# Attention, top-1 experts and a Winograd-form feed-forward on one core: the last stage's block sums spread over the steps, gates applied to the tokens on ACT, weight conversion given out by a budget of DVE work

## The chip, the core and the metric

One NeuronCore of a Trainium2 chip runs the whole program in one launch; the other cores are idle. The metric is the device time of that launch in microseconds (us). Of the kernel before there are three timed runs, given with their median, and one profiled execution, which has a time of its own.

## The reference, cut to what matters

```python
out = q @ (k^T v)                              # 8 batches, 8 heads, 576 rows, 64 dims, no softmax
x = out / sqrt(mean(out^2) + 1e-6) * g_norm    # 4608 tokens of 512
logits = norm(x) @ norm(expert_emb)^T / tau    # 8 experts
e = argmax(logits); gate = softmax(logits)[e]
x = gate * (relu(x @ w1[e]) @ w2[e])           # 512 -> 1024 -> 512, the token's expert alone
h = x @ w_in;  g = h * cos(h);  y = g @ w_out  # 512 -> 2048 -> 512, every token
```

The second feed-forward's weights come as float64. The gate is a softmax value and so positive.

## The kernel before, in words

Every product that has to be exact is made of three passes over split operands: a high half, and a low half that is the rest (`PASS`, L229). ACT makes the high half by a copy and DVE the low half by a subtraction.

The program has three stages.

1. Attention, normalisation, ranking of the tokens by expert, and scattering of the rows to `xs` in expert order.
2. The expert stage, the loop over `g` at L1347. There are 16 chunks of 304 tokens (`CH`, `NC`), each in 8 positions (`f`), so g = 8c + f. Position g issues `layer1` of (c, f), which is 12 matmuls into a PSUM bank `hps`, with a ReLU on ACT and the low half on DVE; then `layer2` of the position two before, 12 matmuls into the four banks `y`. `turn_x` transposes the next chunk's rows in positions 3 to 6. `gate_x` is a generator that computes the gate of a chunk's rows in small pieces, one a position, on ACT and DVE; it then writes the gates to DRAM and reads them back broadcast to 128 partitions (L208, L212). `store_y` multiplies the four `y` banks by that broadcast gate on DVE (L267) and `flush` stores them to `yT`. `load_x` (L158, POOL's queue) brings the rows `xr` of a chunk. Beside all this the loop converts the float64 weights of the third stage from their bits (`bits`, `convert`, `prepare`), a piece at a time: L1416 says by hand how many pieces a position gets, one to three.
3. The last stage: nine blocks of 512 tokens, each in eight steps, so steps 0 to 71, and two more to drain. The two layers are done in Winograd's form of a 2x2 block product, with seven products in place of eight. Step i (`step`, L1197) issues the seven hidden products of step i into the banks `ha` and `hb` ("h" units), and the six or seven output products of step i - 2 into banks `o_a11`, `o_s2` and so on ("o" and "t" units); `units` (L471) gives the order. Between them DVE and ACT form h cos(h), its sums and their halves. PE must have its `ha` or `hb` read by DVE or ACT before it writes it anew.

A block ends in a step that the code calls `done`. There DVE forms E1 = U2 + s3, a half of the output tile `o_sb`, and U2 + acc; in the first slot of the step after (`after`, L1254) it makes the two remaining sums, and POOL sends four sets of 128 rows to `out` by indirect DMAs (`out_rows`, L1171). After the last step these two sums and four DMAs end the program (L1480). Such an end of a block with the step after it is called a seam below.

```python
            if after:
                ...
                add(o2[:, :, 256:512], halves(E1), halves(bank[prior, "s1"]))
                add(o1[:, :, 256:512], halves(U2), halves(bank[prior, "s1"]))
                out_rows(prior, 0, o1)
                out_rows(prior, 1, o2)
```

Of the kernel before, what the change touches and what calls it, by code (L numbers as in the profile page):

```python
# [10 lines left out]
F32 = mybir.dt.float32  # L11
# [25 lines left out]
def tile_kernel(ctx, tc, q, k, v, g_norm, emb, tau, w1, w2, w_in, w_out, out):  # L37
# [36 lines left out]
    BY_POOL = 3  # L74
# [86 lines left out]
    def gate_x(c):  # L161
# [16 lines left out]
        for r in range(4):  # L178
# [5 lines left out]
            if r % 2:  # L184
# [13 lines left out]
        nc.scalar.activation(out=z, in_=z, func=ACTF.Exp)  # L198
        V.tensor_reduce(out=y, in_=z, axis=AX.X, op=ALU.add)
# [15 lines left out]
    def turn_x(c, k, ps=None):  # L215
        if k == 0:
            c["xT"] = [[P.xt.tile([128, CH], F32R, name=f"xT{a}{q_}", tag=f"xT{a}{q_}") for q_ in range(4)] for a in range(2)]
        p = P.ps_x.tile([128, 512], F32, name="xp", tag="xp") if ps is None else ps()
# [9 lines left out]

    PASS = ((0, 0), (0, 1), (1, 0))  # L229

    def layer1(c, f):
        w = c["w"](f)
        p = P.ps_h.tile([128, 512], F32, name="hps", tag="hps")
# [68 lines left out]
    def bits(raw, t, mk, out):  # L302
        lo, hi = raw[:, :, 0], raw[:, :, 1]
        hf = hi.bitcast(F32)
        nc.scalar.activation(out=mk, in_=hf, func=ACTF.Abs)
# [3 lines left out]
        yield 7  # L309
        V.scalar_tensor_tensor(out=t, in0=hi, scalar=-0x40000000, in1=t, op0=ALU.bitwise_and, op1=ALU.bitwise_or)  # L310
        yield 7
        V.scalar_tensor_tensor(out=out.bitcast(F32), in0=mk, scalar=TINY, in1=t.bitcast(F32), op0=ALU.is_gt, op1=ALU.mult)

    def convert(x):
        layer, m = CONV[x]
        if x == 0:
            convert_load(0)
            convert_load(1)
            for _ in range(4):
                yield 7  # L320
# [6 lines left out]
        yield 7  # L327
# [102 lines left out]
    def prepare(store, a, layer, q_):  # L430
# [7 lines left out]
        if layer == 0:  # L438
            sum_(s1, a21, a22, ALU.add)
            sum_(a21, a11, a21, ALU.subtract)  # L440
            yield 8
            sum_(s2, s1, a11, ALU.subtract)
            sum_(s4, a12, s2, ALU.subtract)
        else:
            sum_(s1, a12, a11, ALU.subtract)
            sum_(s4, a22, a12, ALU.subtract)
            yield 8
            sum_(s2, a22, s1, ALU.subtract)
            sum_(a12, a21, s2, ALU.subtract)
        yield 8  # L450
        t = WAB[0]
        store_some(7)
        for i, n, src in ((0, 2, a[:, 0:512]), (2, 2, a[:, 512:1024]), (4, 3, o)):
            src = src.rearrange("p (n c) -> p n c", n=n)
            split2(t[:, i:i + n, 0], t[:, i:i + n, 1], src)
            yield 3 * n + 1
        for u in range(7):
            if layer and (q_ or u not in KEPT):
# [12 lines left out]
    def units(i):  # L471
# [4 lines left out]
            h(A11, B11), h(S1, T1), o("a11", W11), h(S2, T2), h(S4, B22), o("a22", W4), h(S3, T3), o("s2", V2),  # L476
            h(A12, B21), o("a12", W21), h(A22, T4), *last, o("s3", V3), o("s1", V1),
# [78 lines left out]
    if True:  # L556
# [409 lines left out]
        for t in range(NTILE):  # L966
# [41 lines left out]
            if t == 29:  # L1008
# [6 lines left out]
                P.gs = pool("gs", 2, bctx, side="right")  # L1015
# [12 lines left out]
    if True:  # L1028
# [83 lines left out]
        def out_unit(o, j, name, w, start, stop):  # L1112
            for th in range(2):
                for n, (a, b_) in enumerate(PASS):
                    nc.tensor.matmul(  # L1115
                        out=o[:, th * 256:th * 256 + 256], lhsT=G[j, name][a][:, th * 128:th * 128 + 128], rhs=w[:, b_, 0:256],
                        start=(start and th == 0 and n == 0), stop=(stop and th == 1 and n == 2),
                    )
# [522 lines left out]
```

## Time and profile before

| | us |
|---|---|
| median of three runs | 1373.41 |
| lowest and highest run | 1369.27 and 1378.28 |
| the profiled execution's own time | 1374.12 |
| its span, first to last instruction | 1372.6 |
| mean granted TensorE clock | 0.991 |

The span is what the rows below divide. Busy time of PE is modelled: a matmul's row reaches into the next one's, so a full stretch shows PE busy all the time and says nothing of its rate. What the profile does show is where PE sits idle, and who ended each wait. PEld is PE's weight load; a wait can stand at PE's row, at PEld's, or at both, since one sequencer issues them.

### The profile page before, as it was taken

How to read it: one execution, taken by the hardware profiler on the slowest of the kernel's cores; microseconds unless marked ns; L12 is line 12 of the kernel's file. 1: busy time of each engine (PE TensorE's matmuls, PEld its weight loads, DVE VectorE, ACT ScalarE, POOL GpSimd, SP SyncE). 2: the span in 40 equal slices, each digit the busy share in tenths (PEclk: the TensorE clock that was granted, in tenths of full speed). 3: DMA queues.
4: the chain of work that ended last, by engine and by line, in shares of the span. 5: the costliest groups of instructions: out<-in, count | busy, mean ns of one | idle time of the engine just before them, and what ended most of it. 6: DMA issues, size and time to landing. Idle time of an engine off the chain costs nothing. (4 is left out here: it accounts for less than half of the span.)

```text
span 1372.6 us, 30155 instructions
## 1 busy us (share of the span) xinstructions
PE 1311.9 (96%) x10825; PEld 1283.7 (94%) x10825; DVE 1119.2 (82%) x2551; ACT 795.7 (58%) x1601; POOL 174.1 (13%) x302
## 2 busy tenths in 40 slices
PE   7997799999999999998999999999999999999995
PEld 6876789999999999998999999999999999999995
DVE  2567957899998988977888898888988888898874
ACT  4657435555555454546657666666666657666662
POOL 1244132313221100000000010100101010010101
PEclk9999999999999999999999999999999999999998
DMA  9998485899999998669988888988888888988882
GB/s 272 299 333 253 135 237 170 209 271 267 243 254 252 254 271 258 191 197 354 343 300 291 291 281 265 312 259 294 286 275 293 267 292 276 298 281 261 287 267 88
DMA packets 239749, 361.20 MB, mean 263 GB/s; under 512 B 27148, under 2 KB 117424, under 8 KB 238376
## 3 DMA queue, kind: packets, MB, share of 16 engines
q1 hardware_dynamic: 221928, 295.25, 70.0%
q0 software_dynamic: 17648, 63.91, 14.6%
q8 instruction: 89, 1.46, 0.4%
q14 instruction: 68, 0.56, 0.1%
q10 hardware_dynamic: 16, 0.02, 0.0%
HBM read 301.19 MB, written 57.91 MB: 262 GB/s over the span
## 5 line engine op out<-in xcount | busy, mean ns | idle before, releaser
L237 PE MATMUL hps<-xT,ring 128*128 128x304 f32 x1536 | 243.0, 306 | 6.5 <-DVE xT L226 3.3
L258 PE MATMUL y<-h,ring 128*128 128x304 f32 x1536 | 236.6, 302 | 4.3 <-DVE yo L267 1.6
L237 PEld LDWEIGHTS hps<-xT,ring 128*128 128x128 f32 x1536 | 219.6, 189 | 9.8 <-DVE xT L226 5.0
L258 PEld LDWEIGHTS y<-h,ring 128*128 128x128 f32 x1536 | 220.3, 188 | 5.6 <-issue 2.9
L1073 ACT ACTIVATE u<-u,half_pi 128x512 f32<-128x512 f32 x142 | 102.4, 721 | 57.9 <-DVE u L1070 51.7
L1174 POOL DMA_INDIRECT out<-o_sb,perm_i x36 | 39.3, 1091 | 703.0 <-DVE o_sb L1147 535.4
L1067 ACT ACTIVATE u<-h 128x512 int32<-128x512 f32 x142 | 89.8, 632 | 64.0 <-DVE h L1147 53.0
L1070 DVE SCALAR_TENSOR_TENSOR u<-h,u 128x512 f32<-128x512 f32 x142 | 98.1, 691 | 28.7 <-ACT u L1067 24.7
L243 ACT ACTIVATE h<-hps 128x304 fp32r<-128x304 f32 x128 | 53.7, 419 | 108.1 <-PE hps L237 108.0
L1115 PE MATMUL o_a<-ring,hi 128*128 128x256 f32 x568 | 107.8, 282 | 0.0
L1144 ACT ACTIVATE hi<-u 128x512 fp32r<-128x512 f32 x142 | 88.6, 624 | 25.8 <-DVE u L1150 22.8
L1150 DVE TENSOR_TENSOR lo<-u,hi 128x512 fp32r<-128x512 f32 x142 | 97.2, 685 | 0.0
L141 DVE TENSOR_TENSOR ring<-raw,ring 128x1024 fp32r<-128x1024 f32 x72 | 87.6, 1216 | 7.0 <-ACT ring L140 6.0
L1144 ACT ACTIVATE hi<-h 128x256 fp32r<-128x256 f32 (+1 forms) x142 | 73.8, 520 | 23.5 <-DVE h L1267 20.0
L1115 PEld LDWEIGHTS o_a<-ring,hi 128*128 128x128 f32 x568 | 87.1, 189 | 0.0
L1267 DVE TENSOR_TENSOR h<-h,u 128x512 f32<-128x512 f32 x71 | 49.0, 690 | 45.4 <-ACT u L1073 45.2
L1115 PE MATMUL o_a<-ring,lo 128*128 128x256 f32 x284 | 79.6, 280 | 0.0
L1150 DVE TENSOR_TENSOR lo<-h,hi 128x256 fp32r<-128x256 f32 (+1 forms) x142 | 78.3, 551 | 0.0
L140 ACT ACTIVATE ring<-raw 128x1024 fp32r<-128x1024 f32 x72 | 75.9, 1054 | 0.8 <-DMA raw<-in_moe_w 0.7
L244 DVE SCALAR_TENSOR_TENSOR h<-hps,h 128x304 fp32r<-128x304 f32 x128 | 59.6, 466 | 15.4 <-ACT h L243 15.3
L1115 PE MATMUL o_s<-ring,hi 128*128 128x256 f32 x372 | 70.0, 282 | 0.0
L1105 PE MATMUL ha<-ring,wb 128*128 128x256 f32 x390 | 58.3, 285 | 1.9 <-DVE h L1147 0.9
(323 smaller groups left out, 3222.7 us busy)
## 6 DMA issues: line engine op xcount, KB each, us to landing
wb<-ws SPq DMA_DIRECT2D x223, 256.0 KB
wa<-ws SPq DMA_DIRECT2D x167, 256.0 KB
raw<-in_moe_w SPq DMA_DIRECT2D x144, 256.0 KB
ring<-ws SPq DMA_DIRECT2D x114, 256.0 KB
wb<-wo SPq DMA_DIRECT2D x97, 256.0 KB
ring<-wo SPq DMA_DIRECT2D x74, 256.0 KB
wa<-wo SPq DMA_DIRECT2D x73, 256.0 KB
ws<-wa POOLq DMA_DIRECT2D x56, 256.0 KB
```

Source lines behind the costliest of these rows:

```text
L140: nc.scalar.activation(out=w[:, 0], in_=raw, func=ACTF.Copy)
L141: nc.vector.tensor_tensor(out=w[:, 1], in0=raw, in1=w[:, 0].bitcast(F32), op=ALU.subtract)
L237: nc.tensor.matmul(out=p[:, 0:CH], lhsT=w[:, a, k * 128:(k + 1) * 128], rhs=c["xT"][b_][k], start=(n == 0), stop=(n == 11),)
L244: V.scalar_tensor_tensor(out=lo, in0=p[:, 0:CH], scalar=0.0, in1=hi.bitcast(F32), op0=ALU.max, op1=ALU.subtract)
L258: nc.tensor.matmul(out=c["y"][d][:, 0:CH], lhsT=w[:, a, 512 + d * 128:512 + (d + 1) * 128], rhs=h[b_], start=(f == 0 and i == 0), stop=(f ...
L1067: nc.scalar.activation(out=n, in_=p, func=ACTF.Copy, scale=TURN, bias=0.25)
L1070: V.scalar_tensor_tensor(out=u, in0=p, scalar=TURN, in1=n, op0=ALU.mult, op1=ALU.subtract)
L1073: nc.scalar.activation(out=u, in_=u, func=ACTF.Sin, scale=2 * math.pi, bias=half_pi)
L1105: nc.tensor.matmul(out=out, lhsT=w[:, a, k * 128:(k + 1) * 128], rhs=x[xi][:, b_, k * 256:(k + 1) * 256], start=(start and n == 0), stop=( ...
L1115: nc.tensor.matmul(out=o[:, th * 256:th * 256 + 256], lhsT=G[j, name][a][:, th * 128:th * 128 + 128], rhs=w[:, b_, 0:256], start=(start an ...
L1144: nc.scalar.activation(out=out, in_=in_, func=ACTF.Copy)
L1150: V.tensor_tensor(out=out, in0=x, in1=y, op=ALU.subtract)
```

## The change

- The order of the output units becomes a11, s2, a12, s3, a22, s1. The sums of a block are put into five slots of two steps, and the last step is a function of its own, `last_step`, which goes over the tokens' two halves and sends each half's rows when it is done.
- From chunk 4 on the gate is multiplied into the token rows `xr` by ACT before they are transposed, instead of into `y` by DVE; ReLU lets a positive factor through. The gate's way through DRAM is gone for these 12 chunks, and `store_y` becomes four ACT copies. `gate_x` and `load_x` of a chunk start earlier (`GATE_AT`, `LOAD_AT`).
- `layer1` and `turn_x` take banks `hps` and `xp` in turn (`any_bank`) from g = 16 on.
- Conversion is given out by a budget: 32 units of DVE work a position, less what the rest of the position needs. ACT's `Abs` stands later within a piece, and 14 weight stores go by SP's queue in place of POOL's.

```diff
@@ gate_x
         V.tensor_scalar(out=mx, in0=n2, scalar1=1e-30, scalar2=None, op0=ALU.max)
+        if SCALED <= c["n"] < NC:
+            yield
         nc.scalar.activation(out=y, in_=mx, func=ACTF.Ln)
...
+        if SCALED <= c["n"] < NC:
+            yield
+            for r in range(4):
+                nc.scalar.activation(out=t[:, r, 0:DM], in_=t[:, r, 0:DM], func=ACTF.Copy, scale=gt[:, r:r + 1])
+            return
@@ store_y
-            V.tensor_tensor(out=o[d], in0=c["y"][d][:, 0:CH], in1=c["gate"], op=ALU.mult)
+            if "gate" in c:
+                V.tensor_tensor(out=o[d], in0=c["y"][d][:, 0:CH], in1=c["gate"], op=ALU.mult)
+            else:
+                nc.scalar.activation(out=o[d], in_=c["y"][d][:, 0:CH], func=ACTF.Copy)
@@ turn_x and layer1
+    turn = [-1]
+
+    def any_bank(name):
+        if turn[0] >= 0:
+            turn[0] += 1
+            name = ("hps", "xp")[turn[0] % 2]
+        p = P.ps_h if name == "hps" else P.ps_x
+        return p.tile([128, 512], F32, name=name, tag=name)
@@ prepare
-            if layer and (q_ or u not in KEPT):
+            if layer and (q_ or u not in KEPT) or not layer and q_ >= 6:
                 stores.append((store[u], t[:, u].rearrange("p a c -> p (a c)").bitcast(F32)))
@@ units
-            h(A11, B11), h(S1, T1), o("a11", W11), h(S2, T2), h(S4, B22), o("a22", W4), h(S3, T3), o("s2", V2),
-            h(A12, B21), o("a12", W21), h(A22, T4), *last, o("s3", V3), o("s1", V1),
+            h(A11, B11), h(S1, T1), o("a11", W11), h(S2, T2), h(S4, B22), o("s2", V2), h(S3, T3), o("a12", W21),
+            h(A12, B21), o("s3", V3), h(A22, T4), *last, o("a22", W4), o("s1", V1),
@@ step
+        def late_sum(b, t, x):
+            add(OUT[b][t][:, :, 256:512], halves(x), halves(bank[b, "s1"]))
+            for th in range(2):
+                out_row(b, t, th)
...
+        def last_step():
...
+            for th in range(2):
+                part = slice(th * 256, th * 256 + 256)
+                for kind, _, name, w in todo:
...
+                    else:
+                        for t, y in ((1, E1), (0, acc)):
+                            add(OUT[b][t][:, th, 256:512], y[:, part], x)
+                            out_row(b, t, th)
...
             if after:
-                prior = b - 1
-                o1, o2 = OUT[prior]
-                add(o2[:, :, 256:512], halves(E1), halves(bank[prior, "s1"]))
-                add(o1[:, :, 256:512], halves(U2), halves(bank[prior, "s1"]))
-                out_rows(prior, 0, o1)
-                out_rows(prior, 1, o2)
+                add(E1, U2, bank[b - 1, "s3"])
...
+            if after:
+                late_sum(b - 1, 1, E1)
...
+            if after:
+                late_sum(b - 1, 0, Y["acc"])
...
             if done:
-                add(E1, U2, bank[b, "s3"])
-                add(OUT[b][1][:, :, 0:256], halves(E1), halves(bank[b, "a22"]))
-                add(U2, U2, Y["acc"])
+                add(Y["acc"], U2, Y["acc"])
@@ the loop over g
+        preps, GATE_AT, LOAD_AT = [], {0: 0, OPEN + 2: 1, OPEN + 5: 2, 2 * OPEN: 3, 2 * OPEN + 3: 4}, {OPEN + 3: 3, 2 * OPEN: 4}
+        for n in range(5, NC):
+            GATE_AT[8 * n - 14] = LOAD_AT[8 * n - 17] = n
+        spare, FULL, CARRY = 0, 32, 15
+
+        def vector_work(c, f, splits):
+            w = 4 + 12 * splits + (6 if c >= NC - 2 else 14 if c == 2 else 0) + (16 if f == 1 and c < 5 else 0)
+            return w + (4 if 3 <= f < 7 else 0) + ({2: 4, 3: 28, 4: 2, 6: 10, 0: 5}.get(f, 0) if c < NC - 2 else 0)
...
+                spare = min(spare, CARRY) + FULL - vector_work(c, f, splits)
+                spent = 0
+                while spare - spent >= 3 and spent < 15:
+                    k = next(conv, 999)
+                    spent += abs(k)
+                    if k < 0:
+                        break
+                spare -= spent
```

DVE at the second seam, before: `e` is E1, `u_8713` is U2, `o_sb` the output tile, `sx` a sum for the next block's tokens, and the rest is the step's own work.

```order
L1147 TENSOR_TENSOR e_8712<-u_8713,o_s_10182 128x512
L1147 TENSOR_TENSOR o_sb_11185<-e_8712,o_a_10120 128x2x256
L1147 TENSOR_TENSOR u_8713<-u_8713,acc 128x512
L1070 SCALAR_TENSOR_TENSOR u_11228<-h,u_11228 128x512
L1147 TENSOR_TENSOR u_11165<-h 128x256
L1150 TENSOR_TENSOR lo_11241<-h,hi_11240 128x256
L1147 TENSOR_TENSOR o_sb_11185<-e_8712,o_s_10190 128x2x256
L1147 TENSOR_TENSOR o_sb_11184<-u_8713,o_s_10190 128x2x256
L376 TENSOR_TENSOR sx<-sx,xb_10946 128x512
L1267 TENSOR_TENSOR h<-h,u_11228 128x512
```

The same place now (E1 is `e_8724`, U2 is `u_8725`).

```order
L1169 TENSOR_TENSOR acc<-u_8725,acc 128x512
L1089 SCALAR_TENSOR_TENSOR u_11238<-h,u_11238 128x512
L1169 TENSOR_TENSOR u_11176<-h 128x256
L1172 TENSOR_TENSOR lo_11251<-h,hi_11250 128x256
L1169 TENSOR_TENSOR e_8724<-u_8725,o_s_10166 128x512
L395 TENSOR_TENSOR sx<-sx,xb_10958 128x512
L1325 TENSOR_TENSOR h<-h,u_11238 128x512
```

Ahead of the step's first own row (L1070, now L1089) stands one sum instead of three, and ahead of `sx` one instead of two.

DVE in the third and fourth slot of the same step, before: `h<-two,hb`, `h<-five,ha` and `h<-one,hb` are the reads of PE's banks.

```order
L1147 TENSOR_TENSOR h<-two,hb 128x256
L1150 TENSOR_TENSOR u_11228<-h,u_11228 128x256
L1150 TENSOR_TENSOR lo_11239<-h,hi_11238 128x512
L1150 TENSOR_TENSOR lo_11243<-u_11165,hi_11242 128x512
L1147 TENSOR_TENSOR h<-five,ha 128x256
L1147 TENSOR_TENSOR h<-one,hb 128x256
L1070 SCALAR_TENSOR_TENSOR u_11338<-h,u_11338 128x512
```

And now:

```order
L1169 TENSOR_TENSOR h<-two,hb 128x256
L1172 TENSOR_TENSOR u_11238<-h,u_11238 128x256
L1172 TENSOR_TENSOR lo_11249<-h,hi_11248 128x512
L1169 TENSOR_TENSOR o_sb_11197<-e_8724,o_a_10194 128x2x256
L1172 TENSOR_TENSOR lo_11253<-u_11176,hi_11252 128x512
L1169 TENSOR_TENSOR h<-five,ha 128x256
L1169 TENSOR_TENSOR o_sb_11197<-e_8724,o_s_10202 128x2x256
L1169 TENSOR_TENSOR h<-one,hb 128x256
L1089 SCALAR_TENSOR_TENSOR u_11335<-h,u_11335 128x512
L1169 TENSOR_TENSOR o_sb_11196<-acc,o_s_10202 128x2x256
```

One sum has come in ahead of `h<-five,ha`, one behind it, and one behind the `u` that follows `h<-one,hb`.

The end of DVE's program now, the second half of the last step (before, the eight sums there were of 128x512, the last two behind the last matmul's bank).

```order
L1169 TENSOR_TENSOR acc<-acc,hb 128x256
L1169 TENSOR_TENSOR u_8725<-e_8724,o_s_18381 128x256
L1169 TENSOR_TENSOR o_sb_19239<-e_8724,o_a_18404 128x256
L1169 TENSOR_TENSOR acc<-u_8725,acc 128x256
L1169 TENSOR_TENSOR e_8724<-u_8725,o_s_18430 128x256
L1169 TENSOR_TENSOR o_sb_19240<-e_8724,o_a_18458 128x256
L1169 TENSOR_TENSOR o_sb_19240<-e_8724,o_s_18466 128x256
L1169 TENSOR_TENSOR o_sb_19239<-acc,o_s_18466 128x256
```

The sums are half as wide, and only the last two need the bank that the last matmuls write.

ACT in the expert stage now, around positions 0 to 2 of a chunk: `h` is the ReLU, `yo` the copies of the finished chunk, `xr<-xr,gt` the gate's scaling of the next chunk and `gx<-xr` the squares of the one after.

```order
L259 ACTIVATE h_5494<-hps 128x304
L286 ACTIVATE yo<-y_5147 128x304
L286 ACTIVATE yo<-y_5148 128x304
L286 ACTIVATE yo<-y_5149 128x304
L286 ACTIVATE yo<-y_5150 128x304
L140 ACTIVATE ring_5518<-raw 128x1024
L364 ACTIVATE wa<-sa 128x2x256 x2
L364 ACTIVATE wa<-sb 128x3x256
L210 ACTIVATE xr<-xr,gt 76x512 x4
L259 ACTIVATE h_5544<-xp 128x304
L328 ACTIVATE c_mk<-c_raw 128x512
L174 ACTIVATE gx<-xr 76x512 x4
```

The `yo` and `xr` rows are new on ACT; between the two ReLUs stand eight instructions more than without them.

## Rows read from the trace of the kernel before

**Rows 1.** The page, busy time, share of the span and instructions of each engine.

```profile
PE 1311.9 (96%) x10825; PEld 1283.7 (94%) x10825; DVE 1119.2 (82%) x2551; ACT 795.7 (58%) x1601; POOL 174.1 (13%) x302
```

**Rows 2.** Stretches: length, PE, PEld, DVE, ACT, POOL busy, clock, DMA share, GB/s.

```profile
185.00:570.00 385.00, 382.10 (x2827) 380.14 (x2826) 340.50 (x799) 201.38 (x388) 73.75 (x139) 1.00 0.88 242
570.00:600.00 30.00, 28.04 (x204) 27.58 (x203) 27.12 (x79) 13.39 (x31) 0.00 (x0) 1.00 0.43 130
600.00:640.00 40.00, 35.85 (x263) 34.89 (x263) 27.14 (x62) 21.28 (x44) 3.85 (x7) 0.96 0.96 325
...
725.00:1357.30 632.30, 627.48 (x5201) 621.35 (x5200) 542.35 (x1076) 403.66 (x800) 30.71 (x28) 1.00 0.84 276
1357.30:1372.60 15.30, 0.00 (x0) 0.00 (x0) 2.46 (x4) 0.00 (x0) 3.90 (x4) 0.67 0.19 73
```

**Rows 3.** Waits of PE, 185 to 600 us: in total, times, longest us.

```profile
PE hps L237 <- DVE xT L226: 2.1, 5, 0.8
PE y L258 <- DVE yo L267: 1.6, 3, 1.1
PE y L258 <- ACT ring L382: 1.2, 1, 1.2
```

**Rows 4.** Waits of PE, 600 to 725 us.

```profile
PE hb L1105 <- DVE h L1147: 0.9, 1, 0.9
PE ha L1105 <- DVE h L1147: 0.9, 1, 0.9
```

**Rows 5.** Waits of PEld, 725 to 1360 us, the seams.

```profile
PEld hb L1105 <- DVE h L1147: 4.1, 6, 0.7
PEld ha L1105 <- DVE lo L1150: 2.7, 7, 0.4
PEld ha L1105 <- ACT h L1144: 1.9, 7, 0.3
```

**Rows 6.** Timeline of the second seam: start, length, engine, operation, [idle before].

```profile
796.53 0.72 ACT L1073 ACTIVATE u<-u,half_pi 128x512 f32<-128x512 f32 x1
...
797.09 0.68 DVE L1147 TENSOR_TENSOR o_sb<-e,o_s 128x512 f32<-128x512 f32 x1
...
798.28 0.68 DVE L376 TENSOR_TENSOR sx<-sx,xb 128x512 f32<-128x512 f32 x1
...
798.88 0.68 DVE L1267 TENSOR_TENSOR h<-h,u 128x512 f32<-128x512 f32 x1
...
800.28 0.41 DVE L1147 TENSOR_TENSOR h<-two,hb 128x256 f32<-128x256 f32 x1
...
802.16 0.41 DVE L1147 TENSOR_TENSOR h<-five,ha 128x256 f32<-128x256 f32 x1
```

**Rows 7.** Timeline of the end.

```profile
1356.95 0.28 PE L1115 MATMUL o_s<-ring,lo 128*128 128x256 f32 x1
...
1359.08 0.68 DVE L1147 TENSOR_TENSOR o_sb<-u,o_s 128x512 f32<-128x512 f32 x1
1360.03 0.97 POOL L1174 DMA_INDIRECT out<-o_sb,perm_i  x1 [64.17 <-DVEq L1513]
...
1363.87 0.97 POOL L1174 DMA_INDIRECT out<-o_sb,perm_i  x1 [0.30 <-issue]
```

**Rows 8.** Groups by line, 185 to 590 us: busy us, mean ns of one, idle before.

```profile
L243 ACT ACTIVATE h<-hps 128x304 fp32r<-128x304 f32 x115 | 48.3, 420 | 96.2 <-PE hps L237 96.1
...
L174 ACT ACTIVATE gx<-xr 76x512 f32<-76x512 f32 x60 | 32.8, 623 | 0.0
...
L225 ACT ACTIVATE xT<-xp,g 128x304 fp32r<-128x304 f32 x56 | 28.1, 503 | 5.4 <-PE xp L220 5.3
...
L267 DVE TENSOR_TENSOR yo<-y,gate 128x304 f32<-128x304 f32 x56 | 22.5, 462 | 4.0 <-DMA gate<-gates 4.0
```

**Rows 9.** Tile xr: durations, then first and last start.

```profile
L158 POOL DMA_DIRECT2D xr<-xs x16: 536/542/635, 133.6 to 526.7; - x16
...
L220 PEld LDWEIGHTS kvp<-ident,xr x8: 138/141/142, 139.7 to 141.6; 76*128 76x128 f32 x8
```

More of the change, by code (lines that the diff above doesn't have):

```diff
@@ L319, in convert @@
             for _ in range(4):
[L320 removed]
+                yield 2
         raw = cv.pop(x)
@@ L1113, in out_unit, with out_half, kept @@
             for th in range(2):
[L1114 to L1118, printed above, removed]
+                out_half(o, j, name, w, th, start and th == 0, stop and th == 1)
+        def out_half(o, j, name, w, th, start, stop, **kw):
+            for n, (a, b_) in enumerate(PASS):
+                nc.tensor.matmul(
+                    out=o[:, th * 256:th * 256 + 256], lhsT=G[j, name][a][:, th * 128:th * 128 + 128], rhs=w[:, b_, 0:256],
+                    start=(start and n == 0), stop=(stop and n == 2), **kw,
+                )
+        def kept(q, w):
+            if q == 0:
+                return WAB[0][:, w]
+            i = KEPT.index(w)
+            return WOUT[q][:, :, i * 256:i * 256 + 256]
         def out_product(u):
@@ L1169, in two_of, with out_row @@
             return x.rearrange("p (n c) -> p n c", n=2)
-        def out_rows(b, t, o):
-            for th in range(2):
-                n = 4 * b + 2 * t + th
-                ins = nc.gpsimd.indirect_dma_start(
-                    out=out, out_offset=bass.IndirectOffsetOnAxis(ap=perm_i[:, n:n + 1], axis=0),
-                    in_=o[:, th], in_offset=None, bounds_check=NT - 1, oob_is_err=False,
-                )
-                tc.add_to_no_dep_group("rows", ins.ins)
-                tc.declare_no_dep(ins.ins, group="rows", reason="every token has its own row")
+        def out_row(b, t, th):
+            n = 4 * b + 2 * t + th
+            ins = nc.gpsimd.indirect_dma_start(
+                out=out, out_offset=bass.IndirectOffsetOnAxis(ap=perm_i[:, n:n + 1], axis=0),
+                in_=OUT[b][t][:, th], in_offset=None, bounds_check=NT - 1, oob_is_err=False,
+            )
+            tc.add_to_no_dep_group("rows", ins.ins)
+            tc.declare_no_dep(ins.ins, group="rows", reason="every token has its own row")
         def halves(x):
@@ L1415, in tile_kernel @@
             if g >= START:
-                for _ in range(1 if splits and (g < 5 * OPEN or f in (0, 1, 7)) else 3 if not splits and 1 < f < 7 or g > 112 and f not in (7, 0) else 2):
-                    next(conv, None)
+                spare = min(spare, CARRY) + FULL - vector_work(c, f, splits)
[6 more added lines that the diff above has]
+                spare -= spent
             if g >= LAG and f2 == 0 and 0 < c2 < NC:
@@ L1420, in tile_kernel @@
             if c < NC:
[L1421 to L1424 removed]
+                preps = [p for p in preps if next(p, preps) is not preps]
+                if c != 1 and c + 1 < NC:
+                    for k in {4: (0,), 5: (1, 2), 6: (3,)}.get(f, ()) if c == 3 else (f - 3,) if 3 <= f < 7 else ():
+                        turn_x(chunks[c + 1], k)
     bctx.close()
+    turn[0] = -1
     cctx, mctx = ctx.enter_context(ExitStack()), ExitStack()
```

110 lines of the change are left out of this document (60 added, 50 removed).

## The prediction

> **What bounds the kernel now.** I read the page's busy times first, then stretches, then the waits of PE and PEld in each stretch, then the timeline where the waits stand. The page says PE 96% [rows 1], and no instruction of PE is removed by the change, so only PE's idle time can be won. The stretches show how little there is of it: 185 to 600 us, most of the expert stage, has 415 - 382.1 - 28.0 = 4.9 us; 600 to 640 us, where the stages meet, 4.2 us; 725 to 1357 us, most of the last stage, 4.8 us; and behind 1357.3 us PE does nothing for 15.3 us [rows 2]. What ended these waits is DVE nearly each time. In the expert stage PE waits for the low halves of the turned tokens (`xT`), for `yo`, which empties the `y` banks, and once for a row of ACT: 4.9 us [rows 3]. Later it waits at the seams for the readers of `ha` and `hb`: 4.1 + 2.7 + 1.9 = 8.7 us at PEld [rows 5]. PE's own rows show less of that, since a matmul's modelled end reaches into the gap; I take PEld's.
>
> **The change, part by part.**
>
> *The end.* The last matmul ends at 1356.95 + 0.28 = 1357.2. Before, DVE ends at 1359.8, POOL starts 0.27 us later, and four issues at (1363.87 - 1360.03) / 3 = 1.28 us end at 1364.8; 7.8 us of landing and closing follow [rows 7]. Now two of the four DMAs go while the second half of the tokens is computed. Behind the last matmul DVE has two sums of 256 columns at about 0.42 us (the length of such a sum [rows 6]) and up to one that is late: the first is done at some 1358.0, POOL starts at 1358.3, and its second issue ends at 1358.3 + 1.28 + 0.97 = 1360.5. That is 4.3 us less. Least: two issues fewer, 2.6 us, if DVE is no sooner; most: 4.9 us, if nothing is late. I take 4.3.
>
> *The seams.* At the second seam the cosine ends at 796.53 + 0.72 = 797.25, but DVE takes up the product that waits for it only at 798.88, behind sums of the old block; `h<-two,hb` comes at 800.28 and `h<-five,ha` at 802.16 [rows 6], and PE has waited for both. Back-to-back sums of 512 columns start 0.60 us apart (798.28 to 798.88). The change takes two ahead of the step and one of two in its first slot, 1.8 us in all; the cosine caps what this brings at 798.88 - 797.3 = 1.6 us. So `h<-two,hb` comes at 798.7, and the first wait, 0.68 us of it, goes. One sum then comes in ahead of `h<-five,ha`: 802.16 - 1.6 + 0.6 = 801.2, done at 801.6. PE stood 0.68 + 0.39 us before its bank was free at 802.6, so without the waits it asks at 801.5: 0.1 of 0.39 us stays. The next sum stands ahead of `h<-one,hb` and holds up the chain to ACT's copy that the third wait is for: 0.28 becomes about 0.4. A seam so goes from 1.35 to 0.5, six seams by 0.85 make 5.1 us; the first and the last seam, whose waits differ, I give nothing. Most: all 8.7. Least: nothing gained and 0.6 us lost at each of the eight seams, 4.8 us, if one of the sums that now come later holds up a reader in every one. I take 5.
>
> *The expert stage.* DVE loses 12 x 4 multiplications of 462 ns, 22.2 us; ACT gains 48 copies, which I price as its ReLU of the same shape, 420 ns, and 48 scalings of 76x512, priced as the squares of that shape plus what a factor by row adds: 623 + (503 - 420) = 706 ns; 20.2 + 33.9 = 54.1 us [rows 8]. In 185 to 600 us DVE goes from 367.6 us (89%) to 345.4 (83%), ACT from 214.8 (52%) to 268.9 (65%) [rows 2]. Neither becomes the bound on average. That ACT makes the `yo` takes away PE's waits for it, and DVE's room takes those for `xT`. But ACT's work is bunched: in positions 1 and 2 it has two ReLUs, four copies, a weight copy, four scalings and four squares, 0.8 + 1.7 + 1.1 + 2.8 + 2.5 = 8.9 us, against two positions of 24 matmuls at 382.1 / 2827 = 0.135 us, 6.5 us. (The weight copy is put at 1.1 us, between two squares' length and less than one pair.) It runs 2.4 us late there, and more where weights are split as well. A position's ReLU is wanted two positions later, 6.5 us, so this stays hidden, with little to spare in a chunk where both come. Of the 4.9 us I take 3.5 as gone. Ends: all 4.9 gone; or a wait of 0.5 us in each of 12 chunks is new and nothing gone, 6 us lost.
>
> The Trainium skill speaks against this move: its page "ScalarE: Activation LUTs", section "Rules for kernel authors", gives multiplications and the like to VectorE and not to ScalarE. By that rule the copies would be dearer on ACT; here the rows have ACT 420 ns against DVE's 462 for the same 128x304 from PSUM [rows 8], so the trace does not bear it out, and it matters only if ACT becomes what PE waits for, the slower case below.
>
> *Loads of tokens.* From chunk 5 on `xr` is loaded three positions ahead of its first use, 9.7 us, where it was eight. The first such load was issued at 133.6 and used at 139.7 [rows 9], so 6.1 us was enough there. I cost it at nothing; the cover is 3.6 us and the slack above.
>
> *Where the stages meet.* Four `yo` sums leave DVE at the end of step 0 and four copies stand on ACT ahead of `one<-ha`, which PE waits for. DVE had 2 x 0.9 us of waits here [rows 4], and the clock's mean over the 40 us is 0.96 [rows 2]: (1 - 0.96) x 40 / 0.5 = 3.2 us at the lower level, 1.2 GHz, which cost 1.6. I take nothing: 1.7 us put on ACT for 1.8 taken off DVE. Ends: 3.4 us won, both; or 1.7 lost.
>
> *The rest.* 22 small DMAs leave SP's queue and two POOL's; 14 weight stores go from POOL to SP, which waits on DVE for each pair at most as it did for the second layer's; conversion has the same instructions, moved to positions with room on DVE. Alternating banks give `layer1` a wider rotation, but no row shows PE waiting for a bank in this stretch. Nothing, with DVE's idle 11% as cover.
>
> **The sum.** 4.3 + 5 + 3.5 = 12.8 us. The profiled execution took 1374.1, so 1361.3; the median of the runs shown stands 0.7 us lower, and I say 1360.6. A change under 1%, 13.7 us, can hardly be told from none here.
>
> **Rivals.**
> - *The seams keep their waits, only later ones* (0.16): the late sums fall before the next readers of `ha` and `hb`. For it: the block's sums are still five, four of them now in one step. Against: DVE has 14% idle there [rows 2]. 4.3 + 3.5 won: 1365.6.
> - *Only the end is won* (0.12): ACT's bunches give back what DVE lost as well. 1369.1.
> - *Everything is won* (0.18): all of the stage's 4.9, the seams' 8.7, the end's 4.3 and the 3.4 where the stages meet, 21.3 us: 1352.1. For it: all of these waits are DVE's. Against: the cosine cap at the seam, and ACT's place in front of `one`.
> - *Slower* (0.08): an `xr` load that lands late. ACT and DVE take their queues in order, and behind the squares stand the ReLUs. It decides from a load of about 9.7 + 4 = 14 us; one of 16 us holds PE for 2 us, 12 chunks for 24. With seams and end still won: 1374.1 - 9.3 + 24 - 0.7 = 1388. For it: the loads share the DMA engines at 88% [rows 2]. Against: 6.1 us [rows 9].
>
> **How the numbers follow.** The forecast has 0.46, and with its own errors of some 3 us in each of three terms runs from 1355 to 1366; a little under half of it lies over 1% faster (below 1359.7), 0.21, and with "everything" and a rest 0.40. Slower by over 1% is the late load, 0.08. The rest, 0.52, is within 1%. The range leaves out the slower case, 0.08, and the outer part of "everything": 1351 to 1372.
>
> **What would show it.** Right: behind the last matmul two indirect DMAs in place of four; PEld's waits in the last stage at some 3.5 us in place of 8.7; no `yo` among PE's waits, ACT busy some 54 us more. Wrong: PE waiting for ACT's rows (`yo`, ReLU) or for `xr` in the expert stage, DVE rows of late sums just ahead of a wait of PE, or the lower clock anywhere new.

## The result, and the profile after

The changed kernel took 1356.82 us (median of 4 runs, 1356.46 to 1358.06), the kernel before beside it 1373.47 (4 runs, 1369.27 to 1378.28): a ratio of 0.988, 95% interval 0.985 to 0.991. In a later series it took 1364.33 us (6 runs, 1358.66 to 1366.29) against 1378.82 (17 runs), 0.989, interval 0.987 to 0.991. So it is faster by 0.9 to 1.5%. Where the time went is read by stage, from the two profiled executions, whose spans are 1355.5 us and, before, 1372.6.

The page's busy times [rows 1]:

```profile
PE 1302.9 (96%) x10825; PEld 1279.5 (94%) x10825; DVE 1102.2 (81%) x2511; ACT 846.2 (62%) x1698; POOL 175.4 (13%) x286
```

ACT has 50.5 us more, DVE 17.0 less, POOL as much as before. Stretches (columns as in [rows 2]); the first is the expert stage in one piece:

```profile
185.00:600.00 415.00, 410.03 (x3025) 407.48 (x3024) 354.13 (x831) 265.16 (x517) 67.04 (x126) 1.00 0.78 234
600.00:640.00 40.00, 34.63 (x260) 33.61 (x259) 23.79 (x49) 20.77 (x45) 2.20 (x4) 0.96 0.88 297
725.00:1345.00 620.00, 616.45 (x5152) 614.30 (x5151) 536.36 (x1071) 401.47 (x793) 40.31 (x29) 1.00 0.86 279
1345.90:1355.40 9.50, 0.00 (x0) 0.00 (x0) 1.11 (x4) 0.00 (x0) 2.52 (x3) 0.65 0.29 109
```

PE idles 415 - 410.0 = 5.0 us in the expert stage, where it idled 4.9; 5.4 us where the stages meet, after 4.2; 3.6 us in the last stage, after 4.8; and the rest behind the last matmul is 9.5 us long instead of 15.3. Waits of PE, 185 to 600 us [rows 3]:

```profile
PE xp L253 <- DVE xT L233: 2.4, 4, 0.7
PE y L274 <- DVE yo L284: 1.3, 1, 1.3
PE xp L227 <- DVE xT L233: 0.7, 1, 0.7
PE hps L253 <- DVE xT L233: 0.5, 1, 0.5
```

The waits for `yo` are down to one, in a chunk that DVE still multiplies; those for `xT` rose from 2.1 to 3.6 us. The sum is 4.9 us, as before. Waits of PE, 600 to 725 us, the three longest [rows 4]:

```profile
PE o_s L1124 <- DMA wa<-ws: 2.6, 1, 2.6
PE ha L1124 <- ACT one L1166: 1.0, 1, 1.0
PE ha L1124 <- DVE h L1169: 0.9, 1, 0.9
```

One of DVE's two waits became one for ACT. The 2.6 us are for weights that a DMA brings; all such waits here come to 3.7 us, after 3.1. Waits of PEld in the last stage, up to 1345 us [rows 5]:

```profile
PEld o_s L1137 <- PE o_a L1137: 4.7, 7, 0.7
PEld ha L1124 <- ACT ring L401: 0.3, 1, 0.3
```

All three waits of a seam are gone, and a new one is there. PE's own rows have it too, as the only line of that stretch:

```profile
PE o_s L1137 <- DVE o_sb L1169: 3.5, 7, 0.5
```

The timeline at one seam shows whose it is (it answers to [rows 6]). `five`, and below `one` and `two`, are ACT's copies out of the banks `hb` and `ha`; `u<-u,half_pi` is the cosine; `sx` and `xb` belong to the next block's tokens, which `pump` brings up piece by piece:

```profile
1114.56 0.38 ACT L1166 ACTIVATE five<-hb 128x256 f32<-128x256 f32 x1 [0.33 <-PE hb L1124]
1114.84 0.71 ACT L1092 ACTIVATE u<-u,half_pi 128x512 f32<-128x512 f32 x1
1114.98 0.68 DVE L395 TENSOR_TENSOR sx<-sx,xb 128x512 f32<-128x512 f32 x1
1115.58 0.69 DVE L1325 TENSOR_TENSOR h<-h,u 128x512 f32<-128x512 f32 x1
...
1121.32 0.68 DVE L1169 TENSOR_TENSOR o_sb<-acc,o_s 128x512 f32<-128x512 f32 x1
...
1122.14 0.47 PE L1137 MATMUL o_s<-wa,hi 128*128 128x256 f32 x2 [0.49 <-DVE o_sb L1169]
```

PE's last unit of the step writes the bank `s1`, and DVE has only just read it for the old block: the second late sum runs to 1122.0. The end [rows 7]:

```profile
1345.56 0.28 PE L1137 MATMUL o_s<-ring,lo 128*128 128x256 f32 x1
...
1346.70 0.41 DVE L1169 TENSOR_TENSOR o_sb<-acc,o_s 128x256 f32<-128x256 f32 x1
1347.06 0.98 POOL L1195 DMA_INDIRECT out<-o_sb,perm_i  x1 [0.61 <-DVE o_sb L1169]
1348.35 0.98 POOL L1195 DMA_INDIRECT out<-o_sb,perm_i  x1 [0.30 <-issue]
```

Two issues stand behind the last matmul, and POOL is done 1349.3 - 1345.8 = 3.5 us after it, where it took 1364.8 - 1357.2 = 7.6.

The same program points in every trace make the comparison. The table gives us between starts. Positions 16 and 127 are those of the loop over g (first matmul of `layer1`); the first column runs from the start of the span, not from position 0. Steps are those of the last stage (first product's first matmul), "last matmul" is its end, and "issue" is the end of POOL's last output issue.

| kernel | start to pos. 16 | 16 to 127 | step 0 to 8 | 8 to 66 | 66 to last matmul | to last issue | to the end |
|---|---|---|---|---|---|---|---|
| before | 211.4 | 394.7 | 84.7 | 593.5 | 71.2 | 7.6 | 7.8 |
| changed, first | 205.3 | 395.0 | 85.5 | 587.3 | 71.0 | 3.5 | 6.2 |
| changed, again | 213.8 | 395.1 | 84.4 | 587.3 | 71.0 | 3.5 | 6.2 |
| whole last step | 204.7 | 395.8 | 85.4 | 587.3 | 71.0 | 7.1 | 6.3 |
| old seams | 211.2 | 395.5 | 85.2 | 594.0 | 71.2 | 3.5 | 6.6 |
| old expert stage | 208.8 | 395.7 | 86.7 | 587.6 | 71.0 | 3.5 | 8.1 |
| `s1` early | 206.2 | 395.6 | 83.5 | 590.3 | 71.3 | 3.5 | 6.5 |
| old pacing | 210.0 | 423.0 | 84.1 | 587.1 | 71.0 | 3.5 | 7.9 |
| one bank each | 214.3 | 395.3 | 84.4 | 588.1 | 71.0 | 3.5 | 6.1 |
| gate at the end | 207.9 | 405.9 | 84.5 | 587.0 | 71.0 | 3.5 | 6.5 |
| no piece | 205.2 | 395.4 | 85.1 | 612.7 | 71.0 | 3.5 | 6.2 |
| late loads | 204.0 | 398.8 | 87.0 | 586.9 | 71.0 | 3.5 | 6.0 |
| both moves | 209.7 | 395.2 | 85.2 | 615.5 | 71.3 | 3.5 | 6.5 |
| early cosine | 209.5 | 395.3 | 85.3 | 582.4 | 70.6 | 3.5 | 6.2 |

### The profile page after: what moved, and what is told of

Same layout as the page of the kernel before. It is cut to its first block, busy times and chain, and to the rows that moved or that the text cites. A ratio compares the mean times of both kernels' runs of the same rounds, so it can differ in the third digit from the quotient of the medians.

```text
span 1355.5 us, 30321 instructions
## 1 busy us (share of the span) xinstructions
PE 1302.9 (96%) x10825; PEld 1279.5 (94%) x10825; DVE 1102.2 (81%) x2511; ACT 846.2 (62%) x1698; POOL 175.4 (13%) x286
## 4 chain that ended last, share of the span: by engine, by line
PE 66%; DVE 11%; issue 9%; DMA 5%; ACT 4%; SPq 3%; POOL 1%; POOLq 0%; ACTq 0%; DVEq 0%
PE ha L1124 12%; PE y L274 10%; PE hb L1124 9%; PE o_s L1137 9%; PE o_a L1137 9%; PE hps L253 7%; PE hb L1137 3%; PE xp L253 3%; DMA vr<-in_v 1%; DMA wa<-ws 1%; SPq L599 1%; DVE gx L180 1%; DVE ring L141 1%; DVE o_sb L1169 1%; ACT gx L174 1%
## 5 line engine op out<-in xcount | busy, mean ns | idle before, releaser
L253 PE MATMUL hps<-xT,ring 128*128 128x304 f32 x1152 | 182.8, 308 | 2.7 <-DVE xT L233 1.8
L253 PEld LDWEIGHTS hps<-xT,ring 128*128 128x128 f32 x1152 | 165.0, 190 | 4.1 <-DVE xT L233 2.2
L1195 POOL DMA_INDIRECT out<-o_sb,perm_i x36 | 48.6, 1350 | 684.8 <-DVE o_sb L1169 576.5
L1089 DVE SCALAR_TENSOR_TENSOR u<-h,u 128x512 f32<-128x512 f32 x142 | 97.9, 689 | 24.8 <-ACT u L1086 22.9
L259 ACT ACTIVATE h<-hps 128x304 fp32r<-128x304 f32 x96 | 40.3, 419 | 78.6 <-PE hps L253 74.5
L253 PE MATMUL xp<-xT,ring 128*128 128x304 f32 x384 | 60.1, 303 | 2.4 <-DVE xT L233 2.4
L260 DVE SCALAR_TENSOR_TENSOR h<-hps,h 128x304 fp32r<-128x304 f32 x96 | 44.4, 463 | 18.2 <-ACT h L259 16.3
```

The costliest lines, as they stand in the source:

```text
L253: nc.tensor.matmul(out=p[:, 0:CH], lhsT=w[:, a, k * 128:(k + 1) * 128], rhs=c["xT"][b_][k], start=(n == 0), stop=(n == 11),)
L1089: V.scalar_tensor_tensor(out=u, in0=p, scalar=TURN, in1=n, op0=ALU.mult, op1=ALU.subtract)
```

## The experiments

My theory after the two traces: the end and the seams carry the gain, the expert stage nothing, and the head start up to position 16 is chance. The rival: the gates on ACT and the pacing won it.

**The last step whole again.** The bank-by-bank last step and four sums behind it:

```diff
-            if i == NS + 1:
-                return last_step()
...
-        for i in range(1, NS + 2):
+        for i in range(1, NS + 3):
...
-            step(i)
+            if i < NS + 2:
+                step(i)
+            else:
+                add(E1, U2, bank[NB - 1, "s3"])
+                add(OUT[NB - 1][1][:, :, 0:256], halves(E1), halves(bank[NB - 1, "a22"]))
+                late_sum(NB - 1, 1, E1)
+                late_sum(NB - 1, 0, Y["acc"])
```

> The changed kernel with its last step made whole again: the last products run bank by bank, and the four last sums with their two 128x2x256 adds and four row DMAs come after them (the sums of the seams stay spread, so two more adds stand behind the last product than before). My theory, from the two traces: the time from the last matmul to the end goes back from 9.6 us to the 15.4 us of the kernel before or, by the two adds, 1.2 us more; nothing ahead of the last matmul moves. That is 1356.8 + 5.8 to 7.0 = 1362.6 to 1363.8 us. Rival: the halves only move the waiting ahead of the last matmul (each weight is used for two half passes, and the sums of a half wait for DVE), so the last matmul comes earlier here and the total is within 2 us of the changed kernel, 1355 to 1359.

1364.01 us (6 runs, 1360.79 to 1365.38), 0.992 of before (0.989 to 0.995). Its end:

```profile
1345.65 0.28 PE L1137 MATMUL o_s<-ring,lo 128*128 128x256 f32 x1
...
1348.19 0.98 POOL L1195 DMA_INDIRECT out<-o_sb,perm_i  x1 [59.09 <-DVE o_sb L1169]
...
1352.05 0.98 POOL L1195 DMA_INDIRECT out<-o_sb,perm_i  x1 [0.30 <-issue]
```

From the last matmul to the last issue it takes 7.1 us in place of 3.5, and nothing moves ahead of it: the halves give 3.6 us, and the rival falls. The closing time behind the last issue isn't theirs: it is 6.3 us here with four issues and 8.1 us in the run below with two.

**Old seams.** Order of the units and the sums of [rows 6] put back:

```diff
-            h(A11, B11), h(S1, T1), o("a11", W11), h(S2, T2), h(S4, B22), o("s2", V2), h(S3, T3), o("a12", W21),
-            h(A12, B21), o("s3", V3), h(A22, T4), *last, o("a22", W4), o("s1", V1),
+            h(A11, B11), h(S1, T1), o("a11", W11), h(S2, T2), h(S4, B22), o("a22", W4), h(S3, T3), o("s2", V2),
+            h(A12, B21), o("a12", W21), h(A22, T4), *last, o("s3", V3), o("s1", V1),
...
             if after:
-                add(E1, U2, bank[b - 1, "s3"])
+                late_sum(b - 1, 1, E1)
+                late_sum(b - 1, 0, U2)
```

> The changed kernel with the sums at the seams put back: order of the units as before, both sums of the bank s1 in the first slot of the next step, the last step by halves kept. My theory, from the two traces: the three waits of each seam come back and the one on the bank s1 (0.65 us, eight of them) goes; the eight seams cost 0.8 us each more, so + 6.6 us, 1363.4 us. Rival: the spread sums only traded the waits (the new one of 0.65 us against about 0.7 for the old ones in the fast seams) and the difference between the traces came from elsewhere in those steps: within 1.5 us, 1355 to 1358.5.

1365.54 us (9 runs), 0.994 of before (0.992 to 0.996); steps 8 to 66 take 594.0 us, 6.7 more, and PEld's waits in the last stage are the old ones:

```profile
PEld hb L1124 <- DVE h L1169: 4.1, 6, 0.7
PEld ha L1124 <- DVE h L1169: 2.9, 8, 0.4
PEld ha L1124 <- ACT h L1166: 1.9, 7, 0.3
```

So the spread sums win these and pay with the new wait.

**Old expert stage.** The kernel before with the spread sums and `last_step` alone.

> The kernel before with the spread sums and the last step by halves alone: gates, loads of the tokens, banks and conversion stay as before. My theory: the expert stage gave nothing, the stage meeting lost 1.2 us, and the 6 us that the changed kernel's profiled run was ahead by its 16th position are chance, since the program there is the same up to position 13; so the end and the seams carry the gain, 5.8 + 6.6 = 12.4 us, and 1373.5 - 12.4 = 1361 us, with the median drawn towards 1357 if chance made before's time long. Rival: the gate on ACT and the pacing give 4 to 6 us of the gain; then this kernel takes 1361 to 1363 us, its profiled run passes the positions 16 to 127 slower than the changed kernel, and the 6 us up to position 16 are not won in it. The two are told apart by the stretch from position 16 to 127 in the trace rather than by the median.

1363.31 us (12 runs, 1358.10 to 1371.27), 0.993 of before (0.990 to 0.995). Positions 16 to 127 take 395.7 us with the old gates, banks and pacing, 395.0 and 395.1 with the new: at most 0.7 us. PE waits there 3.1 us for `yo`, 1.2 for ACT's `ring` and 0.7 for `xT`, 5.0 in all; the new stage has the same sum, with more of it on `xT`. The rival's 4 to 6 us aren't in that stretch.

**`s1` read earlier.** One line moved:

```diff
             h(xb, True)
...
             o()
+            if after:
+                late_sum(b - 1, 0, Y["acc"])
             if new:
                 add(h0[:, 0:256], one, xb)
                 parts_of(i, 1)
...
-            if after:
-                late_sum(b - 1, 0, Y["acc"])
```

> The changed kernel with one line moved: the second late sum of bank s1 stands ahead of the add of one and xb and of parts_of in its slot, about 0.9 us earlier on DVE. My theory: the wait of 0.65 us at each of eight seams goes, no wait takes its place since neither of the two operations that it passes frees a bank that PE asks for in that step; 5.3 us less, 1351.5 us. Rival: DVE has no idle time in that step, so PE waits one place later for what was delayed (the next step's first sum through cosine and its product); within 1.5 us, 1355.5 to 1358.

1364.74 us (7 runs), steps 8 to 66 590.3 us: a miss, 3 us slower there. It is the rival's way, PE waiting for what was delayed, but dearer than the wait it replaces. PE's waits in the last stage hold one line:

```profile
PE ha L1124 <- ACT h L1166: 5.0, 7, 0.7
```

The parts that were passed feed the cosine of this slot, and behind that cosine on ACT stands the copy out of `ha` (`h<-ha`), which the next step's first product waits for.

**The changed kernel again.**

> The changed kernel as it is, once more, beside the runs of the other kernels. My theory after the first four: what the change does at the same place in every trace is the seams (-6.2 to -6.6 us between the steps 8 and 66 of the last stage) and the end (-4.1 us between the last matmul and the last issue of POOL), with the expert stage at 0 and the stage meeting at +1; the first 150 us vary by 7 us from run to run with the stretches at half clock. Against 1372 us for the kernel before that makes 1361 to 1363 us, and the 1356.8 us of its first four runs were lucky by some 4. Rival: those four runs are what the kernel takes (1356 to 1358), and each of the variants run so far lost 4 us or more by its own edit.

1364.33 us: the theory's size. The two traces of this one kernel differ ahead of position 16, first (clock 0.99) and again (0.94), from the start to position 16:

```profile
0.00:205.30 205.30, 177.77 (x1857) 161.59 (x1858) 127.78 (x450) 117.10 (x262) 61.51 (x129) 0.99 0.90 258
```

```profile
0.00:213.80 213.80, 188.64 (x1857) 171.46 (x1858) 128.05 (x450) 116.83 (x262) 60.75 (x129) 0.94 0.84 247
```

The same 1857 matmuls are busy 10.9 us longer where more of the stretch has the lower level of 1.2 GHz.

**Old pacing.** Conversion by the old rule; with it ACT's `Abs` stands first in a piece again and the 14 stores are back on POOL's queue:

```diff
-                spare = min(spare, CARRY) + FULL - vector_work(c, f, splits)
...
+                for _ in range(1 if splits and (g < 5 * OPEN or f in (0, 1, 7)) else 3 if not splits and 1 < f < 7 or g > 112 and f not in (7, 0) else 2):
+                    next(conv, None)
```

> The changed kernel with the conversion paced by the old rule (one, two or three pieces in a position), its sign mask taken first as before, and all stores of the first layer's weights on POOL's queue. My theory: the pacing neither gave nor took anything between the positions 16 and 127 (395.0 to 395.8 us in the traces so far), so this kernel stays within 1 us of that there, and the first three steps of the next stage take 30 us instead of 31 to 31.6, since the conversion's last stores land earlier: 0 to -1.5 us in all. Rival: the gates on ACT do win time in the expert stage and the new pacing gives it back; then the positions 16 to 127 take 392 to 393 us here, and the total is 2 to 3 us less.

1391.13 us (5 runs), 1.010 of before (1.008 to 1.012): both theories miss. The waits of PE in positions 16 to 127 and that stretch's busy times:

```profile
PE xp L253 <- DVE xT L233: 11.2, 8, 2.3
PE xp L227 <- DVE xT L233: 8.4, 6, 2.7
```

```profile
210.00:633.00 423.00, 399.06 (x2875) 393.82 (x2873) 338.84 (x792) 250.16 (x492) 71.48 (x131) 0.98 0.71 219
```

DVE is busy 338.8 us there, and in the changed kernel, between the same positions, also:

```profile
205.30:600.30 395.00, 390.03 (x2874) 387.49 (x2874) 338.79 (x792) 252.91 (x492) 63.14 (x117) 1.00 0.77 235
```

The same work for PE and DVE, 28 us apart: PE is idle 23.9 us in place of 5.0, and its matmuls are busy 399.1 - 390.0 = 9.0 us longer, at the lower clock (0.98). DVE ahead of one of the waits, of 1.97 us:

```profile
332.30 0.68 DVE L327 SCALAR_TENSOR_TENSOR c_t<-c_raw,c_t 128x512 int32<-128x512 int32 x1
333.02 0.69 DVE L329 SCALAR_TENSOR_TENSOR c_t<-c_raw,c_t 128x512 int32<-128x512 int32 x1
333.74 0.69 DVE L331 SCALAR_TENSOR_TENSOR sa<-c_mk,c_t 128x512 f32<-128x512 f32 x1
...
335.52 0.19 DVE L198 TENSOR_TENSOR z<-z,tmp 76x32 f32<-76x32 f32 x1
335.63 0.52 DVE L233 SCALAR_TENSOR_TENSOR xT<-xp,g,xT 128x304 fp32r<-128x304 f32 x1
```

Three conversion pieces and, behind them, seven small rows of `gate_x` stand ahead of `xT`. So the wait hangs on what stands ahead of it on DVE, not on DVE's share. What the place of `Abs` and the stores add wasn't tried by itself.

**One bank each.** Without `turn[0] = 0` at g = 16.

> The changed kernel with the banks of the expert stage kept apart again: two for the hidden products, two for the turns. My theory: turns and products rarely ask for a bank at the same time, 395 to 396 us between the positions 16 and 127, total unchanged within 1 us. Rival: with a common rotation the products ride out a late DVE; without it each late copy of the turned tokens stops PE, some 0.3 us at each of twelve chunks, 398 to 400 us there and +3 to +4 us in all.

1364.73 us (4 runs), 395.3 us between the positions: the rotation does nothing there, as I had expected.

**Gate at the end.** `SCALED` out of reach, so that DVE multiplies every chunk's rows (128x304) by the gate, which is loaded some seven positions ahead of its use. `SCALED` also sets where `gate_x` stops, so its pieces fall into other positions too.

> The changed kernel with the gates of the chunks 4 and later applied as before, by DVE, to the finished rows (through the table of gates in memory, loaded 7 positions ahead), instead of ACT scaling the tokens ahead of the turn. DVE gets four products of 128x512 for each of twelve chunks back, ACT loses its four copies and four scalings. My theory: PE has the same stops, 395 to 396 us between the positions 16 and 127, total unchanged within 1 us. Rival: the gates on ACT win the 3.5 us that I forecast for the stage and the pacing or the banks lose it again; then the stretch takes 398 to 399 us here and the total is 3 us more.

1373.12 us (12 runs), 0.996 of before (0.995 to 0.998); 405.9 us between the positions, 10.9 more than the changed kernel: both theories miss. Waits of PE there:

```profile
PE xp L253 <- DVE xT L233: 7.1, 8, 1.8
PE xp L227 <- DVE xT L233: 2.8, 1, 2.8
```

So gates and pacing hang together: with the new pacing and the old place of the gate the stage loses 11 us, with the new place and the old pacing 28, and with both new or both old nothing. Of the 11 us, 4.8 are matmuls that are busy longer (394.8 us; mean clock 0.99). And ahead of the wait of 2.8 us DVE itself had stood 6.96 us for one of ACT's weight copies (`wa`), so the run doesn't say that the products themselves cost this. The Trainium skill's rule that gives `mul` to VectorE ("ScalarE: Activation LUTs", section "Rules for kernel authors") is neither borne out nor refuted by it: with the products on DVE the stretch takes 405.9 us under the new pacing, but 394.7 and 395.7 under the old.

**No piece of the tokens in the step of a seam.** Both calls of `pump` in that step are left out:

```diff
-        for _ in range((0, 1, 3)[min(b, 2)]):
+        for _ in range((0, 1, 2)[min(b, 2)]):
...
-            pump()
+            if not after:
+                pump()
```

> The changed kernel with no piece of the next block's tokens in the step after a seam (one sum of 128x512, 0.68 us of DVE, goes to the step behind it; one empty piece fewer ahead, so that the tokens are done as early). My theory: PE's wait on the bank s1 is DVE's queue being full from the step of the seam on, so 0.6 us less in front of the last late sum takes 0.6 of the 0.65 us at seven of eight seams; 582.5 to 583.5 us between the steps 8 and 66 instead of 587.3, and 4 us less in all than the changed kernel. Rival: as in the run with the sum of s1 moved, another reader is late as soon as this one isn't (ACT's copy of the fourth quarter, wanted at the head of the next step); 587 to 588 us there.

1384.68 us (6 runs): a miss of my own making. With one empty piece fewer, each piece falls into the other slot, and ACT's halves of the tokens come ahead of the copy of `five`. ACT in the step behind a seam, and PE's waits in the last stage:

```profile
804.93 0.63 ACT L401 ACTIVATE xb<-sx 128x512 fp32r<-128x512 f32 x1 [1.13 <-DVE sx L395]
805.47 0.61 ACT L401 ACTIVATE xb<-xb 128x512 fp32r<-128x512 f32 x1
805.98 0.36 ACT L1166 ACTIVATE five<-hb 128x256 f32<-128x256 f32 x1
```

```profile
PE hb L1124 <- ACT five L1166: 13.5, 19, 1.2
PE o_s L1137 <- DVE o_sb L1169: 3.5, 7, 0.5
```

The second line is what counts: DVE did 0.68 us less in a seam's step, and the wait for `s1` is the changed kernel's, to the digit. DVE stood 0.47 us for the cosine instead:

```profile
879.79 0.69 DVE L1327 TENSOR_TENSOR h<-h,u 128x512 f32<-128x512 f32 x1 [0.47 <-ACT u L1092]
```

So a full queue of DVE isn't the cause of the wait for `s1` by itself. I take it to be the cosine, which ACT begins behind `five`; the last run tries that.

**Late loads.** `LOAD_AT[8 * n - 15]` in place of `[8 * n - 17]`.

> The changed kernel with the tokens of the chunks 5 and later loaded one position ahead of their first use instead of three. In the changed kernel's trace 13 to 15 us lie between such a load's issue and the squares, and POOL's copy that waits for the same load came 8.9 us after the issue twice; two positions are 7 us. My theory: the load has landed 6 to 9 us after its issue, so ACT stands 0 to 2 us at each chunk and takes most of it back ahead of what PE asks of it: 395 to 399 us between the positions 16 and 127. Rival, the slower case of the prediction: the loads take as long as 14 us while the queues are full, so that here each holds ACT and through it PE for 6 us and more, some 24 us or more in all, 420 us.

1361.48 us (6 runs), 398.8 us between the positions: 3.8 more, as the theory had it. My slower rival is far off even with one position of cover.

**Both moves**, the missed one and `s1` early.

> The changed kernel with both moves at the seam: no piece of the tokens in the step after it, and the second late sum of s1 ahead of the sum and the parts in its slot. My theory: the first move gives DVE the 0.6 us that the second took from the parts, so neither the bank s1 nor ACT's copy is late: 582 to 583 us between the steps 8 and 66, 1 us less than with the first move alone. Rival: the copy on ACT still comes late, since the cosine ahead of it waits for the parts: 585 to 588 us.

1388.67 us (6 runs), steps 8 to 66 615.5 us: a miss as well. 28.2 us over the changed kernel are the two misses added, 25.4 and 3.0.

**The cosine early**, with the pieces in their slots. Three moves in a seam's step: no piece of the tokens in it, the cosine ahead of `five`, and one difference earlier:

```diff
-            pump()
+            if not after:
+                pump()
...
+            if after:
+                cosine(Y["u", 0])
             if new:
                 copy(five, xb)
...
                 copy(two, xa)
+                if after:
+                    sub(s24[:, 1], r0[:, 1], s24[:, 0])
                 add(h1[:, 0:256], two, xb)
...
```

> The changed kernel with three moves in the step of a seam alone: no piece of the next block's tokens in it (the pieces keep their slots and come one step later), the cosine ahead of ACT's copy of five, and the last of the four differences ahead of the sum of two and xb. My theory, from the rows of the run without a piece: DVE is not late there by a queue that filled up, but from the product with the cosine on; ACT takes the cosine only behind the copy that waits for the product hb, and from there DVE has no gap up to the last late sum. A cosine 0.6 us earlier then takes the wait of 0.65 us on the bank s1 away, at each of eight seams: 582 to 583.5 us between the steps 8 and 66 instead of 587.3, 4 to 5 us less in all. Rival: ACT's copies, the cosine now ahead of them, make PE wait for hb as in the run without a piece (1 us at a seam and at the third step after it): 590 us and more.

1353.96 us (6 runs, 1348.18 to 1357.08), 0.984 of before (0.981 to 0.987): the best of all. Steps 8 to 66 take 582.4 us, 4.9 less than the changed kernel; between 725 and 1345 us PE's own rows have no wait left, and PEld's have two:

```profile
PEld o_s L1137 <- PE o_a L1137: 1.4, 7, 0.2
PEld hb L1124 <- issue: 0.3, 1, 0.3
```

The same seam as above, in this kernel: the cosine comes 1114.88 - 1113.68 = 1.20 us after the step's first matmul, where it came 1114.84 - 1112.92 = 1.92 us after it.

```profile
1114.88 0.71 ACT L1092 ACTIVATE u<-u,half_pi 128x512 f32<-128x512 f32 x1
1115.49 0.38 ACT L1166 ACTIVATE five<-hb 128x256 f32<-128x256 f32 x1
```

The three moves weren't tried one by one. What can be told apart is where they win. At one seam its step and the step behind it (50 and 51, between starts) take 10.71 + 11.15 us before, 10.01 + 10.93 in the changed kernel and 9.54 + 10.72 here. So the changed kernel had a second, smaller loss, 0.21 us in the step behind, which its lists of waits show at no seam but one. There ACT makes two halves of the tokens (L401) ahead of `one<-ha`, and PE writes `ha` anew just after that copy; here ACT has no such halves in that step. I put that part down to the moved piece, and to the wait for `s1` the 0.47 us in the seam's step.

## Why the prediction was right, and where it wasn't

I said 1360.6 us, 1351 to 1372; the kernel took 1356.8 and, in the later series, 1364.3. By its terms:

- *The end, 4.3 us.* Right. Two of four issues behind the last matmul, POOL done after 3.5 us (I had 3.3) instead of 7.6: 4.1 us. The trace's further 1.6 us, of the 7.8 behind the last issue, I hadn't claimed; in the runs that time varies from 6.0 to 8.1, and I see no tie to the edit.
- *The seams, 5 us.* The sum right, the working not. Measured 593.5 - 587.3 = 6.2, and 0.2 behind step 66. By steps, the six whole seams that I counted give 5.2 (0.6 to 0.9 each, for my 0.85), the first one 0.7, and single steps elsewhere the rest. The step that failed is "the next sum stands ahead of `h<-one,hb` and holds up the chain ... 0.28 becomes about 0.4": the old third wait went, and so did all of the second. The wait that remains is for the bank `s1`, 0.67 us at PEld at each seam, because the second late sum was put behind the chain that the cosine feeds; with the cosine earlier (and the two other moves) it costs nothing. I followed the readers of `ha` and `hb`, not the last unit's own bank. The residue forecast at PEld was some 3.5 us; it was 4.7 + 0.3 = 5.0 between 725 and 1345 us. The gain is larger than 8.7 - 5.0, since PEld's rows had shown 1.35 us of the old loss at a seam, and against the run with the early cosine it was 21.86 - 20.26 = 1.60.
- *The expert stage, 3.5 us.* Wrong: 0, at most 0.7. The step is "DVE's room takes those for `xT`. Of the 4.9 I take 3.5 as gone". The durations were right (copy 424 ns for my 420, scaling 716 for 706, in the rows below; ACT is 50.5 us busier for my 54), `yo` did go from the later chunks, but the waits for `xT` grew by 1.5 us and the sum stayed 4.9. I argued from DVE's share; the run with the old pacing has the same work on DVE and takes 28 us more.

```profile
L210 ACT ACTIVATE xr<-xr,gt 76x512 f32<-76x512 f32 x48 | 30.7, 716 | 0.1
L286 ACT ACTIVATE yo<-y 128x304 f32<-128x304 f32 x48 | 19.2, 424 | 0.0
```

- *Loads and banks, 0.* Right: a load two positions later costs 3.8 us, and the rotation changes nothing. *Conversion, 0 with DVE's room as cover*: the cover isn't the room. With the old rule of pacing the stage lost 28 us, and only pacing fitted to the new places of the gates made it nothing.
- *Where the stages meet, 0.* PE's wait passed from DVE to ACT's `one`, as I feared, but steps 0 to 8 took 85.5 and 84.4 us against 84.7: no difference.

The end and the seams make 4.1 + 6.4 = 10.5 us, where I had summed 12.8; the ratios' intervals say 12 to 21 and 13 to 18. So it is partly luck that my number lies between the two medians: the stage that gave nothing was made up for by 4 to 6 us that no term had.

Where these come from isn't settled, but the record narrows it. The two medians of the changed kernel differ by the clock: the runs' mean granted clock has a median of 0.9935 in the first four runs and 0.9885 in the later six, and (1 - clock) x span, my estimate of what the lower level took, is 8.8 and 15.7 us. Between the kernels the clock explains little: in the later series the kernel before has 0.987, 17.9 us by the same estimate, 2.2 more, and 1.7 of that lies behind the last matmul, where the traces show 0.67 over 15.3 us and 0.65 over 9.5 and PE has nothing to do. The kernel before itself took between 1371.95 us (21 runs) and 1378.82 by series. In the series where it took 1371.95, the first four variants come within 3 us of what the table's terms give (at the widest the old seams, 6.4 us won for 3.6). Ahead of position 16 one program can differ by several us: the changed kernel's two traces were 6.1 us ahead of before's single one there and 2.4 us behind it, and the run with the old expert stage, which has before's own program up to there, was 2.6 us ahead. Chance may be all of it; no run decides.

## What to carry to other kernels

Moving work off a crowded engine won nothing here by its share: what counts is which instruction stands ahead of the one that is waited for, and an edit there has to be tried with the pacing it belongs to. When late sums are spread over a step, list every bank that the step writes, its last one too, and follow the chain that feeds the sum back to the other engine: here one activation put ahead of one copy, with two smaller moves, was worth 4.9 us. A wait that is too short for the list of waits still counts: compare the lengths of steps as well. Compare traces between the same program points, since a stage that the edit doesn't touch can differ by more than the edit is worth.

## What I had not expected of the hardware

One kernel's two traces differ by 8.5 us ahead of position 16 (205.3 and 213.8); mean granted clock there is 0.99 and 0.94, and the same matmuls were busy 10.9 us longer. The mean clock alone doesn't give the time: the run with the whole last step has the same program up to there, 0.96 and 204.7 us. And in the two runs with many waits of PE, of up to 2.8 us, parts of the expert stage ran at the lower level of 1.2 GHz (mean 0.98 over 423 us with the old pacing, 0.99 over 405.9 with the gate at the end), where the changed kernel has 1.00.
